# Mixing k and v with tokens on partitions, with crossbar transposes and POOL copies, in a fused attention and feed-forward kernel

## The chip, the cores and the metric

The kernel runs on one core of one Trainium2 chip. The metric is device time in microseconds (us): the median of several executions on the chip. A second number, the span, is the time from the first to the last instruction of one profiled execution, some 2 us shorter.

Engines: PE does matmuls (TensorE), PEld loads their weights, ACT is ScalarE, DVE is VectorE, POOL is GpSimd, SP is the queue that issues most transfers here. Each works off a queue of its own. In this kernel the order on PE, POOL and SP is fixed by hand, and the traces below show POOL and SP keeping to it: a kT copy starts only behind a gate and its loads (at 125.49 us), a transpose of v only behind one of q (at 77.47 us).

## The reference, cut to what matters

```python
B, H, S, D = 4, 8, 768, 64;  n_blocks = 8;  block = 96
P = sort_net                                   # [B, H, 8, 8], five normalising rounds (cut)
k_sorted = einsum('bhij,bhjcd->bhicd', P, k_b) # every block becomes a mix of the 8 blocks
v_sorted = einsum('bhij,bhjcd->bhicd', P, v_b)
scores = scale * q_b @ k_sb.T;  attn = softmax(scores) @ v_sb     # per block of 96 tokens
x = attn as [3072, 512];  out = ((x @ w_a) * (x @ w_b)) @ w_out   # d_ff = 1536
```

## The kernel before

Heads are worked on in pairs: batch `b` has pairs `g = 4b .. 4b+3`. Batch 0 has a path of its own. While PE does the feed-forward of batch `b`, small units of the attention of batch `b+1` are put between its steps. A unit is `c_` (mix k and v), `s_` (scores and exponentials) or `o_` (output). A gate is a POOL copy of one element: POOL waits for its source, and so the loads that follow it in program order are held back. In the views `pf` and `po` are the matmuls of the first and second half of the feed-forward, `mix`, `sc` and `o_ps` those of the three units; `hT` holds what lies between the two halves.

```python
def stage_mix(g, what, engines):               # 12 matmuls, 128 columns each, for k or for v
    mix = psA.tile([P, 2, 512], FP32, tag="A", name="mix")
    for c in range(NCH):                       # NCH = 6
        for e in range(2):                     # the two heads: lower and upper half of the array
            nc.tensor.matmul(mix[e * D:(e + 1) * D, c // 3, c % 3 * P:(c % 3 + 1) * P],
                             lhsT=src2[:, e, c * D:(c + 1) * D], rhs=s_all[:, 2 * g + e], ...)
    ...                                        # copied to kT or vT: d on partitions, tokens along
    if what == "v" and g > HP:                 # HP = 4
        nc.sync.dma_start_transpose(out=vss[g % NBUF][:, :, V0:V0 + P], in_=...)

def c_(g):
    ...
    stage_mix(g, "k", ("act",))
    stage_mix(g, "v", ("dve", "act"))
    if 2 * HP - 2 <= g < B * HP - 2:           # pace the loads of the pair after next
        nc.gpsimd.tensor_copy(out=gate, in_=kTs[g % NBUF][0:1, 0:1])
        load_pair((g + 2) // HP, (g + 2) % HP) # k, v, q: three loads issued by POOL

def s_(g):
    stage_scores(g)
    ...
    pair_q(g + 1)                              # POOL copy of q (qc)
    stage_q(g + 1)                             # crossbar transpose of it (qTf), on SP

for u, n in ((c_, 0), (s_, 0), (c_, 1), (s_, 1), (c_, 2), (o_, 0), (s_, 2), (c_, 3),
             (o_, 1), (s_, 3), (o_, 2), (o_, 3)): ...
```

The softmax here doesn't subtract the row's maximum and nothing guards it: scores larger than these inputs give would overflow.

## Time and profile before

| | before |
|---|---|
| time, median of 3 first runs | 245.47 us (245.16 to 245.64) |
| span of the profiled run | 243.3 us |
| PE busy | 237.4 us, 98% |
| mean granted TensorE clock | 1.0 |
| PE waits in the steady part | 0.2 us |

The page of the kernel before, its busy times (us, share of the span, instructions) and the chain of work that ended last, by engine and by line:

```profile
PE 237.4 (98%) x2309; PEld 141.6 (58%) x2309; DVE 109.1 (45%) x258; ACT 104.4 (43%) x204; POOL 61.4 (25%) x88
...
PE 93%; DVE 4%; ACT 1%; DMA 1%; issue 0%
PE pf L332 52%; PE po L377 24%; PE mix L281 4%; PE o_ps L231 3%; PE sc L302 2%; PE mixh L180 2%; PE po L362 1%; PE vs_ps L208 1%; PE xt_ps L222 1%; PE sc L195 1%; DMA p_nat<-in_sort_net_dram 1%; PE heat L168 1%; PE two L332 1%; PE q_ps L260 1%; DVE xp L237 1%
```

PE is the bound: its instructions fill 93% of the chain. The mixes are 4% of it. Everything else hides behind PE, as long as PE never waits.

The same chain in order of time (start, length, what), at the start of batch 2's attention:

```profile
84.17 1.30 PE pf L332 x8
85.47 0.79 PE mix L281 x24
86.26 2.71 PE pf L332 x16
88.97 0.45 PE sc L302 x16
```

A mix of one pair takes 0.79 us, and the 16 matmuls behind it 2.71 us where 16 undisturbed ones take 2 x 1.30. So a mix costs 0.90 us in all. The scores stand one short stretch of feed-forward behind.

The timeline of POOL of the kernel before, for one mixing unit (start, length, what, and in brackets its idle time before with the releaser):

```profile
102.53 0.18 POOL L542 COPY gate<-kT 1x1 bf16<-1x1 bf16 x1 [4.45 <-ACT kT L162]
103.04 0.72 POOL L95 DMA_DIRECT2D k<-in_k_dram  x1 [0.34 <-PE pf L332]
103.75 0.72 POOL L95 DMA_DIRECT2D v<-in_v_dram  x1
104.46 0.73 POOL L95 DMA_DIRECT2D q<-in_q_dram  x1
105.18 0.85 POOL L246 COPY qc<-q 128x768 bf16<-128x768 bf16 x1
```

From the gate to the end of the third load issue POOL is held for 2.65 us. Before the change no score waits for POOL: kT is written by ACT, and the POOL copies of q come early enough.

### The profile page before, as it was taken

Reading aid. Unit: us, or ns where it says so; the run is one execution under the profiler, and the core shown is the slowest. Engines: PE = TensorE matmul, PEld = TensorE weight load, DVE = VectorE, ACT = ScalarE, POOL = GpSimd, SP = SyncE. Lnnn points to the kernel's source line nnn. Section 1 sums busy time; section 2 is a strip of 40 time slices with the busy share of each in tenths; the row PEclk is TensorE's granted clock in tenths of the full one; section 3 lists DMA queues with packets and bytes.
Section 4 is the critical chain, followed back from the end, with each engine's and each line's share of the span. In section 5 each row is a group of like instructions: output and inputs, shape, how many; then the busy total and the mean of one; then the engine's idle time right before and its main releaser. Section 6 shows DMA issues by size and latency. Waiting matters only on the chain.

```text
span 243.3 us, 5625 instructions
## 1 busy us (share of the span) xinstructions
PE 237.4 (98%) x2309; PEld 141.6 (58%) x2309; DVE 109.1 (45%) x258; ACT 104.4 (43%) x204; POOL 61.4 (25%) x88
## 2 busy tenths in 40 slices
PE   7999999999999999999999999999999999999994
PEld 7776666666554466666654466666654466665442
DVE  6774557555435234464534144363625144344110
ACT  3675853565630175736330165737330133333001
POOL 8766569623220053240400054200000000000000
PEclk9999999999999999999999999999999999999999
DMA  5999999985999589993964369923524310000132
GB/s 78 202 198 196 196 201 201 203 138 83 158 204 153 130 70 155 171 138 70 136 115 122 115 120 114 159 51 58 47 75 131 109 43 0 3 0 1 46 129 86
DMA packets 53930, 28.04 MB, mean 115 GB/s; under 512 B 30736, under 2 KB 50960, under 8 KB 53904
## 3 DMA queue, kind: packets, MB, share of 16 engines
q0 software_dynamic: 20944, 14.16, 41.6%
q1 hardware_dynamic: 32816, 13.45, 28.0%
q8 instruction: 18, 0.29, 0.5%
q14 instruction: 8, 0.07, 0.1%
q10 hardware_dynamic: 144, 0.07, 0.1%
HBM read 28.32 MB, written 6.29 MB: 142 GB/s over the span
## 4 chain that ended last, share of the span: by engine, by line
PE 93%; DVE 4%; ACT 1%; DMA 1%; issue 0%
PE pf L332 52%; PE po L377 24%; PE mix L281 4%; PE o_ps L231 3%; PE sc L302 2%; PE mixh L180 2%; PE po L362 1%; PE vs_ps L208 1%; PE xt_ps L222 1%; PE sc L195 1%; DMA p_nat<-in_sort_net_dram 1%; PE heat L168 1%; PE two L332 1%; PE q_ps L260 1%; DVE xp L237 1%
## 5 line engine op out<-in xcount | busy, mean ns | idle before, releaser
L353 DVE TENSOR_TENSOR hT<-a_sb,pf 128x384 bf16<-128x384 bf16 x95 | 52.6, 553 | 73.8 <-PE pf L332 46.4
L332 PE MATMUL pf<-xT,w_a_sb 128*128 128x384 bf16 x380 | 78.0, 326 | 0.2 <-ACT xT L162 0.2
L332 PE MATMUL pf<-xT,w_b_sb 128*128 128x384 bf16 x380 | 77.5, 326 | 0.0
L352 ACT CAST a_sb<-pf 128x384 bf16<-128x384 f32 x95 | 45.5, 479 | 60.9 <-PE pf L332 41.3
L377 PE MATMUL po<-w_out_sb,hT 128*128 128x512 bf16 x276 | 61.9, 379 | 0.0
L332 PEld LDWEIGHTS <-w_b_sb 128*128 128x128 bf16 x384 | 37.5, 98 | 24.8 <-issue 0.3
L332 PEld LDWEIGHTS <-w_a_sb 128*128 128x128 bf16 x384 | 34.9, 98 | 22.2
L377 PEld LDWEIGHTS <-hT 128*128 128x128 bf16 x276 | 26.3, 98 | 30.0
L162 ACT COPY o_sb<-po 128x512 f32<-128x512 f32 (+1 forms) x13 | 7.5, 577 | 46.8 <-PE po L377 45.2
L164 DVE COPY o_sb<-po 128x512 f32<-128x512 f32 (+1 forms) x12 | 7.9, 656 | 35.2 <-PE po L377 26.3
L307 ACT ACTIVATE eT<-sc 96x768 bf16<-96x768 f32 x24 | 18.0, 802 | 6.9 <-PE sc L302 6.9
L542 POOL COPY gate<-kT 1x1 bf16<-1x1 bf16 x8 | 1.4, 179 | 74.7 <-ACT kT L162 74.7
L237 DVE TENSOR_TENSOR xp<-o_ps,rec 96x512 bf16<-96x512 f32 x24 | 15.9, 684 | 0.6 <-DVE rec L235 0.2
L162 ACT CAST kT<-mix 128x384 bf16<-128x384 f32 x24 | 10.3, 482 | 8.0 <-PE mix L281 8.0
L95 POOL DMA_DIRECT2D k<-in_k_dram x16 | 11.6, 724 | 4.5 <-PE pf L332 2.3
L95 POOL DMA_DIRECT2D v<-in_v_dram x16 | 11.5, 721 | 3.1 <-DMA w_b_sb<-in_moe_w_b_dram 1.2
L231 PEld LDWEIGHTS <-eT 96*128 96x128 bf16 x256 | 10.4, 97 | 3.2 <-DVE xp L237 0.6
L235 DVE RECIPROCAL rec<-o_ps 96x8 f32<-96x8 f32 x32 | 5.6, 189 | 13.8 <-PE o_ps L231 13.8
L231 PE MATMUL o_ps<-vs,eT 96*128 96x65 bf16 x256 | 11.3, 193 | 0.2 <-DVE xp L237 0.2
L246 POOL COPY qc<-q 128x768 bf16<-128x768 bf16 x10 | 8.4, 842 | 7.2 <-DMA q<-in_q_dram 7.2
L95 POOL DMA_DIRECT2D q<-in_q_dram x12 | 8.7, 721 | 1.7 <-DMA w_a_sb<-in_moe_w_a_dram 0.7
L168 PE MATMUL heat<-warm 128*128 128x128 bf16 x84 | 7.6, 264 | 1.3 <-DVE warm L77 1.3
(80 smaller groups left out, 158.3 us busy)
## 6 DMA issues: line engine op xcount, KB each, us to landing
out_dram<-o_sb SPq DMA_DIRECT2D x17, 256.0 KB, 2.0
k<-in_k_dram POOLq DMA_DIRECT2D x16, 192.0 KB, 6.0
v<-in_v_dram POOLq DMA_DIRECT2D x16, 192.0 KB, 6.4
q<-in_q_dram POOLq DMA_DIRECT2D x12, 192.0 KB, 6.7
w_a_sb<-in_moe_w_a_dram POOLq DMA_DIRECT2D x6, 256.0 KB, 9.8
w_b_sb<-in_moe_w_b_dram POOLq DMA_DIRECT2D x6, 256.0 KB, 10.0
w_out_sb<-in_moe_w_out_dram POOLq DMA_DIRECT2D x3, 512.0 KB, 10.8
out_dram<-o_sb SPq DMA_DIRECT2D x12, 128.0 KB, 2.4
```

What stands on the lines that cost most here:

```text
L95: nc.gpsimd.dma_start(out=to, in_=_ap(t, base, [[W, P], [S * D, 2], [1, W]]))
L162: nc.scalar.copy(out=out, in_=in_)
L168: nc.tensor.matmul(ps[:, 0:cols], lhsT=warm[:, 0:P], rhs=warm[:, 0:cols], start=True, stop=True)
L231: nc.tensor.matmul(o_ps[:, e, i * (D + 1):(i + 1) * (D + 1)], lhsT=eT[:, hf, e, i * BLK:i * BLK + P], rhs=vs[0:BLK, i0 + i, V0 - 1 + e * ( ...
L237: nc.vector.tensor_tensor(out=_ap(xp, i0 * 2 * D, [[nxp * 2 * D, BLK], [D, 2], [2 * D, NBH], [1, D]]), in0=_ap(o_ps, 1, [[1024, BLK], [511 ...
L246: nc.gpsimd.tensor_copy(out=qc.rearrange("p c e d -> p e c d"), in_=loaded[g][2].rearrange("p e (c d) -> p e c d", c=NCH))
L281: nc.tensor.matmul(mix[e * D:(e + 1) * D, c // 3, c % 3 * P:(c % 3 + 1) * P], lhsT=src2[:, e, c * D:(c + 1) * D], rhs=s_all[:, 2 * g + e], ...
L307: nc.scalar.activation(out=eT[:, hf, :, 0:HB], in_=sc[0:BLK, :, 0:HB], func=AF.Exp, scale=float(scale))
L332: nc.tensor.matmul(pf[:, 0:HW], lhsT=w_sb[:, kc, m * P:(m + 1) * P], rhs=x_cols(b, kc, t), start=(kc == 0), stop=(kc == KA - 1))
L352: nc.scalar.copy(out=a_sb, in_=pf[:, 0:HW])
L353: nc.vector.tensor_mul(out=hT[:, m, t * HW:(t + 1) * HW], in0=a_sb, in1=ab[1][:, 0:HW])
L377: nc.tensor.matmul(held["po"], lhsT=hTs[b][:, m, c * P:(c + 1) * P], rhs=w_out_sb[:, m, :], start=(m == 0), stop=(m == KO - 1))
```

## The change: intent and diff

The intent is to take PE work away. With tokens on partitions one mix is 2 matmuls of 384 columns with the mixing matrix as weights, in place of 12 of 128 columns. The result then has to be turned: k by one crossbar transpose, v by two, and POOL copies put the blocks in order. The mix of the next pair moves ahead of the scores, to give this longer path time. One buffer of hT goes, for space. Core of the diff:

```diff
+    def stage_kv(g):
+        for n, (what, engines) in enumerate((("k", ("act",)), ("v", ("dve", "act")))):
+            ...
+            for e in range(2):
+                nc.tensor.matmul(mix[:, e, 0:W], lhsT=s_all[:, 2 * g + e], rhs=src2[:, e], ...)
+            nat = att.tile([P, NCH, 2, D], BF16, tag="nat", name="nat")
+            ...                                   # copies mix -> nat on ACT, or DVE and ACT
+            nc.sync.dma_start_transpose(out=turned, in_=nat.rearrange("p c e d -> p (c e d)"))
+    def order_kv(g):                              # two POOL copies: turned -> kT, turned -> vT
+        for what, to in (("k", kTs[...]...), ("v", vTs[...]...)):
+            nc.gpsimd.tensor_copy(out=to, in_=st[g, what].rearrange("p c (i t) -> p c i t", i=NB))
+    def return_v(g):                              # the transpose of v that was there before
-            hTs[b] = ffp.tile([P, KO, S], BF16, tag="hT", name="hT")
+            hTs[b] = ffp.tile([P, KO, S], BF16, tag="hT", name="hT", bufs=1)
 def c_(g):
-                stage_mix(g, "k", ("act",))
-                stage_mix(g, "v", ("dve", "act"))
+                if g > HP:
+                    stage_kv(g)
+                else: ...                         # as before
                 if 2 * HP - 2 <= g < B * HP - 2:
-                    nc.gpsimd.tensor_copy(out=gate, in_=kTs[g % NBUF][0:1, 0:1])
+                    nc.gpsimd.tensor_copy(out=gate, in_=st[g, "v", "nat"][0:1, 0, 0, 0:1])
                     load_pair((g + 2) // HP, (g + 2) % HP)
-            for u, n in ((c_, 0), (s_, 0), (c_, 1), (s_, 1), (c_, 2), (o_, 0), (s_, 2), (c_, 3),
-                         (o_, 1), (s_, 3), (o_, 2), (o_, 3)):
+            # (unit, pair, what follows it, for which pair)
+            for u, n, then, m in ((c_, 0, None, 0), (c_, 1, order_kv, 0), (s_, 0, return_v, 0),
+                                  (c_, 2, order_kv, 1), (s_, 1, return_v, 1), (o_, 0, None, 0),
+                                  (c_, 3, order_kv, 2), (s_, 2, return_v, 2), (o_, 1, order_kv, 3),
+                                  (s_, 3, return_v, 3), (o_, 2, None, 0), (o_, 3, None, 0)):
```

It touches 11 pairs: 5 to 15.

More of the change, by code (lines that the diff above doesn't have):

```diff
@@ L290, in stage_mix @@
                 copy(eng, d1, s1)
-        if what == "v" and g > HP:
-            nc.sync.dma_start_transpose(out=vss[g % NBUF][:, :, V0:V0 + P],
-                                        in_=to.rearrange("p i t -> p (i t)"))
+    def stage_kv(g):
+        for n, (what, engines) in enumerate((("k", ("act",)), ("v", ("dve", "act")))):
+            src2 = loaded[g][n]
+            mix = psA.tile([P, 2, 512], FP32, tag="A", name="mix")
+            for e in range(2):
+                nc.tensor.matmul(mix[:, e, 0:W], lhsT=s_all[:, 2 * g + e], rhs=src2[:, e],
+                                 start=True, stop=True)
+            nat = att.tile([P, NCH, 2, D], BF16, tag="nat", name="nat")
+            step = 2 // len(engines)
+            for u, eng in enumerate(engines):
+                copy(eng, nat[:, :, u * step:(u + 1) * step].rearrange("p c e d -> p e c d"),
+                     mix[:, u * step:(u + 1) * step, 0:W].rearrange("p e (c d) -> p e c d", c=NCH))
+            turned = att.tile([P, NCH, P], BF16, tag="turned", name="turned")
+            nc.sync.dma_start_transpose(out=turned, in_=nat.rearrange("p c e d -> p (c e d)"))
+            st[g, what, "nat"], st[g, what] = nat, turned
+    def order_kv(g):
+        for what, to in (("k", kTs[g % NBUF][:, 0:S].rearrange("p (i c t) -> p c i t", i=NB, c=NCH)),
+                         ("v", vTs[g % NBUF][:, :, 0:BLK].rearrange("p i (c t) -> p c i t", c=NCH))):
+            nc.gpsimd.tensor_copy(out=to, in_=st[g, what].rearrange("p c (i t) -> p c i t", i=NB))
+    def return_v(g):
+        nc.sync.dma_start_transpose(out=vss[g % NBUF][:, :, V0:V0 + P],
+                                    in_=vTs[g % NBUF].rearrange("p i t -> p (i t)"))
     def stage_scores(g):
@@ L538, in c_ @@
                     turn_q(g)
-                stage_mix(g, "k", ("act",))
-                stage_mix(g, "v", ("dve", "act"))
+                if g > HP:
+                    stage_kv(g)
+                else:
+                    stage_mix(g, "k", ("act",))
+                    stage_mix(g, "v", ("dve", "act"))
                 if 2 * HP - 2 <= g < B * HP - 2:
-                    nc.gpsimd.tensor_copy(out=gate, in_=kTs[g % NBUF][0:1, 0:1])
+                    nc.gpsimd.tensor_copy(out=gate, in_=st[g, "v", "nat"][0:1, 0, 0, 0:1])
                     load_pair((g + 2) // HP, (g + 2) % HP)
@@ L557, in o_, with run @@
                 to_xT(g)
-            for u, n in ((c_, 0), (s_, 0), (c_, 1), (s_, 1), (c_, 2), (o_, 0), (s_, 2), (c_, 3),
-                         (o_, 1), (s_, 3), (o_, 2), (o_, 3)):
-                us.append(lambda u=u, g=g0 + n: u(g))
+            def run(u, g, then, n):
+                u(g)
+                if then is not None and g0 + n > HP:
+                    then(g0 + n)
+            for u, n, then, m in ((c_, 0, None, 0), (c_, 1, order_kv, 0), (s_, 0, return_v, 0),
+                                  (c_, 2, order_kv, 1), (s_, 1, return_v, 1), (o_, 0, None, 0),
+                                  (c_, 3, order_kv, 2), (s_, 2, return_v, 2), (o_, 1, order_kv, 3),
+                                  (s_, 3, return_v, 3), (o_, 2, None, 0), (o_, 3, None, 0)):
+                us.append(lambda u=u, g=g0 + n, then=then, m=m: run(u, g, then, m))
             return us
```

## The prediction

> **What bounds the kernel now.** TensorE. The page of busy times gives PE 237.4 us of 243.3 (98%); the chain that ended last lies on PE for 93% of the span, and the granted clock is 1.0. The feed-forward matmuls are 76% of that chain (52% pf, 24% po); the k and v mix is 4%. Almost no PE wait is left in it. DVE (45%), ACT (43%) and POOL (25%) have room. So two things count: PE time removed, and new waits of PE.
>
> **What it removes.** For 11 of 12 later pairs, 24 mix matmuls of 128 columns become 4 of 384. Columns streamed hardly change: the old ones run two side by side in column halves. The chain shows 0.79 us for an old pair of mixes, and the 8 pf matmuls behind them take 1.41 us where undisturbed ones take 1.30: 0.90 in all. Eight 384-column matmuls take 1.30, so four should take 0.65. Saving about 0.25 us x 11 = 2.7 us. Evacuations keep their sizes (ACT 0.48, DVE 0.56 us).
>
> **What it adds.** Per pair two crossbar transposes on SP (1.23 us issue; existing ones land in 2.8 us when the DMA is quiet, 5.8 median, up to 7.6 with loads running) and two POOL copies of 128x768 (the like-sized qc copy takes 0.84 us). Single-buffered hT should cost nothing.
>
> **What lies on the critical path.** Not the mean load but the order on POOL. order_kv of pair n-1 is queued behind the next pair's gate and its three load issues. The timeline shows 2.65 us from gate start to the end of the third issue. The gate now waits for DVE's v evacuation, about 1.45 us after the mix starts. So kT is ready about 1.45 + 2.65 + 0.85 = 5.0 us after the next pair's mix starts. The scores that need it are planned only 1, 2 or 3 steps of 1.3 us behind that mix, at 1.95, 3.25 or 4.55 us. Waits: 3.05, 1.75, 0.45 us. Six gated cases: batch 1, 1.75 + 3.05; batch 2, 0.45 + 1.75 + 1.75; batch 3, 0.45. Sum 9.2 us. The DMA is already 90% busy in much of 40 to 110 us; two more transposes a pair make landings later, so the first scores of batch 2 and the last return of v in batch 1 may wait another 1 to 3 us. I take 11 to 12 us of new PE waits.
>
> The Trainium skill (DMA: Bandwidth & Descriptors, "Issuing engine by pattern") lets transposes run only from hardware queues; the trace agrees, all 33 are on SP. So one that waits for POOL holds back those queued behind it.
>
> **Predicted time.** 245.5 - 2.7 + 11.7 = 254.5 us, range 247.5 to 264. Faster by over 2%: 0.02; within 2%: 0.2; slower: 0.78.
>
> **What would show each step.** PE mix per changed pair near 0.65 us, with 1.30 behind it. New idle time of PE or its weight load before the scores, released by POOL's kT copy, 5 to 12 us in about six pieces, in batch 2 at its first three score stages, in batch 3 almost none after the first. POOL busy up about 19 us. Share of the hardware queue up from 28% to about 40%; median landing of transposes above 5 us.
>
> **What would make it wrong.** POOL copies with 16-element runs slower than 0.84 us (each 0.4 us more adds about 2.5 us). Landings so late that DMA holds the scores (worse). The other way: a gate released earlier than I think, or waits that absorb each other, leaves only the PE saving and the time within 2%.

## The result, and the profile after

| | before | after |
|---|---|---|
| time, median | 245.54 us (4 runs) | 259.37 us (257.8 to 262.81, 4 runs, one of them slow) |
| ratio of the fast runs, 95% interval | | 1.0545 (1.0459 to 1.0631) |
| span of the profiled run | 243.3 us | 256.2 us |
| mean granted clock | 1.0 | 0.993 |

All ratios here are taken from fast runs alone, so not quite the ratio of the quoted medians. The mean of the three fast runs is 258.84 us. An execution counts as slow when it is more than 1.5% above the fastest one of its kernel.

The same parts of the page, of the changed kernel:

```profile
PE 235.9 (92%) x2078; PEld 139.2 (54%) x2089; DVE 109.3 (43%) x258; ACT 104.0 (41%) x193; POOL 78.8 (31%) x110
...
PE 73%; DMA 11%; POOL 6%; DVE 4%; issue 2%; ACT 2%; SPq 1%; POOLq 0%; DVEq 0%
```

PE is busy 1.5 us less, yet the span grew by 12.9 us. The chain now runs through DMA and POOL for 17%. So PE waits. Its largest waits in the changed kernel (who waited for whom: us in total, times, longest):

```profile
PE sc L324 <- POOL kT L311: 7.0, 5, 2.9
PE sc L324 <- DMA qTf<-qc: 4.7, 2, 3.4
PE o_ps L231 <- DMA vs<-vT: 2.4, 1, 2.4
```

That is 14.1 us in eight pieces. The timeline of PE of the changed kernel shows where each stands (only the lines with a wait in brackets):

```profile
58.34 0.51 PE L324 MATMUL sc<-qT,kT 64*128 64x96 bf16 x16 [1.66 <-POOL kT L311]
...
68.22 0.51 PE L324 MATMUL sc<-qTf,kT 64*128 64x96 bf16 x16 [2.93 <-POOL kT L311]
...
80.74 0.65 PE L231 MATMUL o_ps<-vs,eT 96*128 96x65 bf16 x16 [2.37 <-DMA vs<-vT]
...
99.92 0.51 PE L324 MATMUL sc<-qTf,kT 64*128 64x96 bf16 x16 [0.36 <-POOL kT L311]
...
111.13 0.82 PE L324 MATMUL sc<-qTf,kT 64*128 64x96 bf16 x16 [3.44 <-DMA qTf<-qc]
...
126.41 0.51 PE L324 MATMUL sc<-qTf,kT 64*128 64x96 bf16 x16 [1.69 <-POOL kT L311]
...
160.58 0.51 PE L324 MATMUL sc<-qTf,kT 64*128 64x96 bf16 x16 [0.38 <-POOL kT L311]
...
169.62 0.52 PE L324 MATMUL sc<-qTf,kT 64*128 64x96 bf16 x16 [1.26 <-DMA qTf<-qc]
```

The first three are in batch 1, the next three in batch 2, the last two in batch 3. The timeline of POOL of the changed kernel, just ahead of the wait at 126.41:

```profile
122.90 0.18 POOL L567 COPY gate<-nat 1x1 bf16<-1x1 bf16 x1 [10.91 <-DVE nat L164]
123.35 0.72 POOL L95 DMA_DIRECT2D k<-in_k_dram  x1 [0.28 <-issue]
124.07 0.72 POOL L95 DMA_DIRECT2D v<-in_v_dram  x1
124.78 0.73 POOL L95 DMA_DIRECT2D q<-in_q_dram  x1
125.49 0.86 POOL L311 COPY kT<-turned 128x768 bf16<-128x768 bf16 x1
```

POOL was idle for 10.91 us before the gate. The kT copy stood in line behind a gate that waits for the mix of the next pair, and behind three load issues.

The chain in order of time of the changed kernel, around the longest wait:

```profile
101.42 9.58 DMA qTf<-qc
...
111.13 0.82 PE sc L324 x16
111.96 5.11 PE pf L354 x24
```

Here a transpose of q took 9.58 us from its issue to its landing. And the 24 matmuls behind the wait took 5.11 us in place of 4.0, the 16 of the scores 0.82 in place of 0.51. The table by stretches explains that (from:to, length, busy time and count of PE, PEld, DVE, ACT and POOL, then the granted clock, the DMA share, which counts packet times and can pass 1, and GB/s):

```profile
111.90:117.00 5.10, 5.10 (x29) 2.83 (x28) 1.11 (x2) 2.71 (x5) 0.09 (x1) 0.78 1.60 160
```

The granted clock was 0.78 there; in 100 to 107 us, up to just before the wait, it was 1.00. The Trainium skill (TensorE: Matmul & The Clock Gate, "What's actually happening") says that an idle window of about 3.4 us takes PE to half clock. This wait of 3.44 us agrees (the clock was 0.50 from 111.13 to 113.0 us); a run below does not.

The mix itself, in the chain of the changed kernel:

```profile
53.43 0.65 PE mix L297 x4
54.08 2.61 PE pf L354 x16
```

0.65 us in place of 0.79, and no 0.11 us lost behind it. The Trainium skill (TensorEngine Tiling (Array Packing), "Key Properties") states that a change of tiling mode drains TensorE. The 0.11 us agrees: it stands behind the mixes that split the array in column halves, and not behind the new ones. The scores, which use half of the rows, are followed by it too: 24 matmuls take 4.01 us behind them, 3.90 behind a new mix (e2). That the drain is its cause is not shown; no run isolates it.

The sum: waits of 14.1 us, less about 2.5 us of mix (measured below), plus 1.4 us at the lower clock (1.1 in the 24 matmuls, 0.3 in the scores before them), make 13.0 us; the span grew by 12.9.

The wait for v has a path of its own. The chain of the changed kernel ahead of it:

```profile
75.43 0.58 SPq L412
...
76.10 1.28 SPq L252
...
77.47 3.13 DMA vs<-vT
```

The POOL copy of this v had ended by 72.94 us. Its transpose was issued at 77.47, behind an output store (L412) and the next q transpose (L252) on SP's queue, and then landed in 3.1 us, as fast as any of v. Issued at once it would have landed at about 76.1 (an estimate from these numbers), and PE asked for it at 78.37. So I read this wait of 2.4 us as one of place on SP's queue, not of a late landing; no run moves that transpose alone.

### The profile page after: what moved, and what is told of

Its sections match the earlier page's. It is cut to its first block, busy times and chain, and to the rows that moved or that the text cites. A ratio compares the mean times of both kernels' runs of the same rounds, so it can differ in the third digit from the quotient of the medians.

```text
span 256.2 us, 5237 instructions
## 1 busy us (share of the span) xinstructions
PE 235.9 (92%) x2078; PEld 139.2 (54%) x2089; DVE 109.3 (43%) x258; ACT 104.0 (41%) x193; POOL 78.8 (31%) x110
## 3 DMA queue, kind: packets, MB, share of 16 engines
q1 hardware_dynamic: 50416, 17.78, 38.7%
## 4 chain that ended last, share of the span: by engine, by line
PE 73%; DMA 11%; POOL 6%; DVE 4%; issue 2%; ACT 2%; SPq 1%; POOLq 0%; DVEq 0%
PE pf L354 38%; PE po L399 22%; DMA qTf<-qc 6%; PE o_ps L231 3%; DMA turned<-nat 2%; PE mix L297 2%; PE sc L324 2%; PE mixh L180 2%; POOL q L95 1%; POOL kT L311 1%; DMA vs<-vT 1%; POOL k L95 1%; PE po L384 1%; PE vs_ps L208 1%; PE xt_ps L222 1%
## 5 line engine op out<-in xcount | busy, mean ns | idle before, releaser
L354 PEld LDWEIGHTS <-w_a_sb 128*128 128x128 bf16 x384 | 36.0, 98 | 23.0 <-issue 0.5
L567 POOL COPY gate<-nat 1x1 bf16<-1x1 bf16 x8 | 1.4, 179 | 69.0 <-DVE nat L164 69.0
L162 ACT CAST nat<-mix 128x768 bf16<-128x768 f32 (+1 forms) x22 | 14.1, 639 | 7.3 <-PE mix L297 5.0
L324 PE MATMUL sc<-qTf,kT 64*128 64x96 bf16 x160 | 5.6, 211 | 10.1 <-POOL kT L311 5.4
L324 PEld LDWEIGHTS <-kT 64*128 64x128 bf16 x192 | 4.8, 97 | 16.4 <-POOL kT L311 8.9
L311 POOL COPY kT<-turned 128x768 bf16<-128x768 bf16 x11 | 9.3, 842 | 11.4 <-PE pf L354 10.1
```

The costliest lines, as they stand in the source:

```text
L162: nc.scalar.copy(out=out, in_=in_)
L311: nc.gpsimd.tensor_copy(out=to, in_=st[g, what].rearrange("p c (i t) -> p c i t", i=NB))
L324: nc.tensor.matmul(sc[:, e, i * BLK:(i + 1) * BLK], lhsT=kT[e * D:(e + 1) * D, blk * BLK:blk * BLK + P], rhs=qT[e * D:(e + 1) * D, :, blk ...
L354: nc.tensor.matmul(pf[:, 0:HW], lhsT=w_sb[:, kc, m * P:(m + 1) * P], rhs=x_cols(b, kc, t), start=(kc == 0), stop=(kc == KA - 1))
```

## The experiments

Two theories stood against each other for the waits. A: the place on POOL's queue; the kT copy stands behind the next pair's gate and loads. B: the crowded DMA; transposes land late beside the loads, whatever the order. C, a relative of A, says the q transposes are late because of where their copy stands on POOL. Eleven kernels ran. e1, e4, e5 and e6 ran on one chip, with 245.07 us before (7 runs).

### e1: the block-order copies ahead of gate and loads

```diff
 def c_(g):
     ...                                # stage_kv
+    if g > HP + 1 and g % HP > 0:
+        order_kv(g - 1)
     if 2 * HP - 2 <= g < B * HP - 2:   # gate, load_pair
-(c_, 1, order_kv, 0) (c_, 2, order_kv, 1) (c_, 3, order_kv, 2)
+(c_, 1, None, 0)     (c_, 2, None, 1)     (c_, 3, None, 2)
```

> The changed kernel with one move: on POOL the two block-order copies of the pair before go ahead of the gate and the three load issues, not behind them. Theory A (order on the POOL queue: 2.65 us of gate and load issues stand between the gate and the kT copy): the five waits of the scores for POOL's kT copy, 7.0 us in the profile of after, go nearly all; the waits for the q transposes (4.7 us) and for v (2.4 us) stay; about 251 us (249 to 253.5). Rival B (the DMA is crowded, transposes land late whatever the order on POOL): the waits come back with the landing of the transposes as the releaser, and the time stays at 256 or above.

Measured: 252.19 us (251.45 to 252.78, 4 fast runs), ratio 1.0287 (1.0263 to 1.0311). The waits of PE:

```profile
PE o_ps L231 <- DMA vs<-vT: 3.5, 1, 3.5
PE sc L324 <- POOL kT L311: 2.3, 1, 2.3
PE sc L324 <- DMA qTf<-qc: 1.8, 1, 1.8
PE sc L324 <- POOL qc L246: 1.7, 1, 1.7
```

The time is A's. The excess over before fell from 5.45% to 2.87%. Four of the five waits for kT are gone; the one left is in batch 1, where the copy itself had waited 3.98 us for the transpose to land. So A holds for these waits. About 9 us of waits remain, all behind transposes from SP's queue. The profile puts one of them, 1.7 us, down to the q copy, but that copy is for the pair after; the q transpose which those scores need landed 6.0 us after its issue, at 108.9 us, just ahead of them (109.09). So it is a q wait too.

### e4: e1 without the later loads (wrong result)

```diff
-                    load_pair((g + 2) // HP, (g + 2) % HP)
+                    loaded[g + 2] = loaded[(g + 2) % HP + HP]
```

> Wrong result on purpose: e1 with the eight later loads of k, v and q left out (pairs 8 to 15 use the data of pairs 4 to 7), so that neither their issues nor their DMA traffic is there; all transposes stay. Theory A: the loads' harm was their place on the POOL queue, which e1 has already mended, so this is within 1.5 us of e1. Rival B: with the loads' traffic gone the transposes land in about 3 us instead of 5 to 12, all waits for q and v go too, and the time falls to 243 to 245, 6 us or more below e1.

Measured: 245.54 us (245.0 to 246.12), ratio 1.001 (0.9984 to 1.0035), so 6.7 us under e1. One wait of the steady part is left, 2.4 us for v. The issues of the profile (what, queue, count, median us to landing):

```profile
turned<-nat SPq DMA_TRANSPOSE x22, 2.8
...
vs<-vT SPq DMA_TRANSPOSE x11, 3.1
qTf<-qc SPq DMA_TRANSPOSE x10, 2.8
```

Without the loads the new transposes land in 2.8 us; in the changed kernel their median was 5.3 and the longest 12.8. So B holds for most of what e1 left: this is the half that A does not explain. e4 takes the load issues from POOL's queue as well as the traffic; e7 parts the two. B had the wait for v go too, and that failed: it is as long as in the changed kernel, with the transposes of v landing in 3.1 us. Even so the kernel only draws level with before: the v wait of batch 1 and moments at a lower clock (0.992 in the profile) eat the saving.

### e7: the changed kernel, POOL copies in place of the loads (wrong result)

```diff
                     nc.gpsimd.tensor_copy(out=gate, in_=st[g, "v", "nat"][0:1, 0, 0, 0:1])
-                    load_pair((g + 2) // HP, (g + 2) % HP)
+                    for _ in range(3):
+                        nc.gpsimd.tensor_copy(out=pad, in_=q_first[:, 0:2, 0:320])
+                    loaded[g + 2] = loaded[(g + 2) % HP + HP]
```

> Wrong result on purpose: the changed kernel in its own order, its later loads replaced by three POOL copies of 128x640 (about 0.73 us each by the 0.84 us of a 128x768 one), so POOL is held as long at the same place but the loads' traffic is gone. The counterpart of e4 (no loads, order mended: 245.5). Theory A, that the place on POOL costs by itself: the waits for POOL's kT copy return in full, 1.7, 2.9, 0.4, 1.7, 1.7 and 0.4 us, about 8 us in sum, and with the v wait that e4 kept the time is 251 to 255. Rival B, that only the loads' traffic hurts: within 1.5 us of e4, 244 to 247.

Measured, where before was 245.05 us (11 runs): 253.01 us (251.19 to 254.75), ratio 1.0318 (1.0276 to 1.0359). It was run at another time. A stand-in copy took 0.716 us, a load issue 0.72. The waits of PE:

```profile
PE sc L325 <- POOL kT L312: 6.5, 4, 2.6
PE o_ps L232 <- DMA vs<-vT: 2.3, 1, 2.3
```

A's waits are back, 6.5 us of them (1.28, 2.58, 1.33 and 1.33; about 8 expected, and the two of 0.4 did not come), with no later load traffic at all. The last but one is the wait that the q transpose hid in the changed kernel. Theory B, that only the traffic hurts, falls. But there is no wait for q any more, although the copy of q for the second scores of batch 2 starts as late (5.4 us after the mix of its own pair starts, 5.7 in the changed kernel): the q transposes land in 2.7 to 2.9 us. So the q waits come from the traffic, not from the place of the copy. C falls in that form, B holds for q.

One line goes against the page quoted above. After a wait of 2.58 us (before 67.82) the clock was low:

```profile
67.80:72.00 4.20, 4.07 (x27) 2.09 (x29) 0.56 (x1) 1.98 (x3) 3.10 (x4) 0.59 0.42 77
```

After the 2.35 us for v it was 0.50 from 81.9 to 85 us. In the changed kernel waits of 2.93 and 2.37 us left the clock at 1.00. So a wait shorter than 3.4 us may or may not cost clock. The runs do not show what decides it.

### e5: q earlier on top of e1

```diff
+                if 2 * HP <= g and g + 1 < B * HP:
+                    pair_q(g + 1); stage_q(g + 1)    # behind order_kv, ahead of gate and loads
```

(and taken out of `s_`).

> e1 with the q copy and the q transpose of the next pair moved up as well: ahead of the gate and loads, one mixing stage earlier than before. Theory C (the q transposes come late because their copy waits on POOL's queue behind block-order copies that wait for landings, and behind load issues): the two q waits of 4.7 us go, 3 to 5 us less than e1, about 247. Rival B (landings limited by the DMA): the q transposes are issued earlier but land as late, time as e1 within 1.5 us.

Measured: 249.14 and 252.51 us in fast runs, two slow ones at 252.9 and 253.0; ratio 1.0233 (1.0151 to 1.0314), called unclear. It doesn't settle C.

### e10: q earlier alone, in the changed kernel

The same move without e1, so q goes ahead of gate, loads and the block-order copies.

> The changed kernel with the q copy and q transpose of the next pair moved ahead of the gate and loads, one mixing stage earlier; the block-order copies stay behind the loads. Theory C (the two q waits, 4.7 us, come from where the q copy stands on POOL, behind loads and block-order copies): the waits for q transposes go, the hidden wait for the kT copy in the second scores of batch 2 comes out at about 1.7 us, the other kT waits stay at 1.7, 2.9, 0.4, 1.7 and 0.4; about 3 us less than the change, 256 (254.5 to 258). Rival B (transposes land late wherever they are issued): q waits of 3 us or more stay, time 257.5 to 261 as the change itself.

Measured: 274.15 us (4 runs, one of them slow), ratio 1.1166 (1.1126 to 1.1207), far outside both expectations. The timeline of POOL:

```profile
97.21 0.72 POOL L95 DMA_DIRECT2D q<-in_q_dram  x1
105.28 0.82 POOL L246 COPY qc<-q 128x768 bf16<-128x768 bf16 x1 [7.35 <-DMA q<-in_q_dram]
...
108.31 0.84 POOL L311 COPY kT<-turned 128x768 bf16<-128x768 bf16 x1
```

I had moved the q copy so early that it waits for a load issued just ahead of it. POOL stood still for 7.35 us with the kT copy in line behind, and PE waited 8.21 us for it (22.0 us for kT copies in all). No wait for q is left, so one half of C's expectation came true, but the edit changed more than the thing it was to test. As a test of C it is void; as a measurement of what a blocked head of a queue costs it is clear.

### e6: the loads moved to the end of each batch

e5, with the four pairs of the next batch loaded in the last four units (`o_1, s_3, o_2, o_3`) of the batch before.

> e5 with the later loads taken out of the mixing stages: the four pairs of the next batch are loaded during the last four units of the batch before, when fewer transposes run. Same number of instructions and bytes as the change. If queue order and the overlap of loads with transposes together are the whole loss, PE waits of stages are under 1.5 us in sum and the time is that of before less the saving of the mix, 242.5 to 245. If rival B holds in the sense that five transposes a pair are too many for the DMA at any time, waits of 3 us or more remain and it is over 248.

Measured: 261.34 us (4 runs, one of them slow), ratio 1.0635 (1.0576 to 1.0694): worse than the change, and neither theory's figure. In the profile all waits of scores are gone, as A and B both ask. Two new ones took their place; the chain in order of time shows the first:

```profile
71.44 10.44 DMA vs<-vT
...
82.01 1.04 PE o_ps L231 x16
83.05 11.49 PE po L399 x42
```

Three loads of 192 KB were issued in the 2.3 us ahead of this transpose of v, and six more while it ran; it landed after 10.44 us, and PE waited 8.3 us. Then 42 matmuls took 11.49 us, where the same 42 take 9.07 in the kernel before: from 82 to 95 us the granted clock was 0.78. The second wait, 4.7 us, is for an xT transpose among the loads for the batch after that (11.33 us). The Trainium skill (DMA: Bandwidth & Descriptors, "Issuing engines are not separate DMA queues") says that transfers of all queues run on the same 16 DMA engines and interleave. This trace agrees: a transpose from SP's queue took 10.44 us among loads from POOL's, 3.1 in e4 without. I read from it that what counts for a transpose is how much load is in flight around it. No run changes the burst alone; e8 below, which spreads the same bytes, changes other things too.

### e2 and e3: the saving, and the rest of the change, by themselves

e2 is the kernel before with the new matmul shape for pairs 5 to 15 and nothing else (wrong result):

```diff
+        if g > HP:
+            for e in range(2):
+                nc.tensor.matmul(mix[:, e, 0:W], lhsT=s_all[:, 2 * g + e], rhs=src2[:, e], ...)
+        else: ...                       # the 12 matmuls as before
```

> Wrong result on purpose: the kernel before with one edit, the mixes of pairs 5 to 15 done as 4 matmuls of 384 columns; copies, transposes, order of units and hT buffers as before. It measures the saving by itself. My sum: 0.90 - 0.65 = 0.25 us a pair, 11 pairs, 2.7 us less: 242.4 (241.9 to 243.0). Rival: PE streams the same columns, so no saving beyond 0.5 us: 244.5 or more.

Measured: 242.65 us (242.43 to 243.16), ratio 0.9899 (0.9882 to 0.9916). The span fell from 243.3 to 240.8. So the saving is real, 2.4 to 2.5 us, some 0.22 us a pair. With no wait added, it is also the most that this change could have given: 1%.

e3 is the kernel before with the new order of units and one hT buffer.

> The kernel before with the change's order of units (the mix of the next pair ahead of the scores) and the single hT buffer, and nothing else. I expect no cost: 245.1 plus or minus 0.7. If the order of units or the hT buffer were a cause of the loss, it is 247 or more.

Measured: 245.74 us in the median of 8 runs, ratio 1.0019 (1.0001 to 1.0036). Six runs lie at 245.26 to 246.25; of the other two 247.78 counts as fast and 250.04 as slow. Mostly as expected: not a cause of 5%. Its profile is of the slow run, so it explains no time. But it shows that a q transpose can be late without the new transposes: the one for the second scores of batch 2 took 10.46 us, and PE waited 2.54 us. The new order of units puts the loads of two pairs, six, ahead of that transpose, where the kernel before has three (5.8 us to landing there). How much of the q waits of the changed kernel is due to that is untested.

### e8, e9, e11: a version that beats both

If A and B are both right, the new mix pays where its long path has time, its copies stand first on POOL, and loads come in small doses. e8 takes the new path for batches 2 and 3 only (8 pairs), and loads one tensor a unit:

```diff
 def c_(g):
+    if g >= 2 * HP:
+        stage_kv(g)
+        if g % HP > 0: order_kv(g - 1)           # first on POOL
+        pair_q(g); stage_q(g)
+    else: ...                                    # as before the change, old order of units
+todo = {2: [[(10, 0), (10, 1)], [(10, 2)], [(11, 0)], ...], 3: [[(14, 1)], [(14, 2)], ...]}
+# after unit j: a gate on that unit's own result, then load_one(pair, k or v or q) for todo[j]
```

> A try at a version that beats both: the new path for batches 2 and 3 only (8 pairs, so batch 1 with its short stages is as before), block-order copies ahead of everything else on POOL, q copy and transpose in the pair's own mixing stage, and the later loads issued one tensor a unit, not three or more at once. If both causes (place on POOL, bursts of loads ahead of transposes) are right, waits of PE at scores and outputs sum to under 1 us and the time is that of before less 8 x 0.25 us: 243.2 (242.5 to 245). If the DMA as such is too full for five transposes a pair beside loads, waits for q, k or v landings of 3 us or more stay and it is over 246.

Measured: 245.81 us, ratio 1.0036 (1.0009 to 1.0063). Only 2.0 us of waits were left, both for the q transpose of a batch's first pair. e9 moves those to the end of the batch before:

```diff
 def o_(g):
+    if g % HP == HP - 1 and g + 1 < B * HP:
+        pair_q(g + 1); stage_q(g + 1)
-todo = {2: [[(10, 0), (10, 1)], [(10, 2)], ...
+todo = {2: [[(10, 0)], [(10, 1), (10, 2)], ...
```

> The spread version again, with the q copy and q transpose of each batch's first pair moved to the end of the batch before (the only PE waits that were left in its profile were 1.81 and 0.20 us, both for the q transpose of a batch's first pair), and one load tensor moved one unit later. If that was all, no PE wait before scores over 0.3 us is left and the time is that of before less 8 x 0.22 us: 243.3 (242.8 to 244.2). If the next transposes in the queue merely take over the wait, 245 or more.

Measured: 244.18 us, ratio 0.9961 (0.9947 to 0.9974). One wait was left, 0.77 us for v of pair 10, the load I had put later. e11 puts that load back:

```diff
-todo = {2: [[(10, 0)], [(10, 1), (10, 2)], ...
+todo = {2: [[(10, 0), (10, 1)], [(10, 2)], ...
```

> The best version so far (244.2) with one load, v of pair 10, issued one unit earlier again, because its profile shows one PE wait of 0.77 us for that load. If the rest stays as it is: 243.4 (243.0 to 244.0), 0.6 to 0.7% under the kernel before. If the two loads side by side push a transpose back into PE's way: 244.2 or more.

Measured: 243.14 us (243.04 to 243.24, 6 fast runs), correct, ratio 0.9912 (0.9897 to 0.9927). The largest waits of PE in its profile:

```profile
PE heat L174 <- DVE warm L77: 1.3, 1, 1.3
PE heat L453 <- DVE rsum L451: 0.4, 2, 0.2
```

The waits that are left lie in the opening, as in the kernel before. It is 2.05 us faster than before (245.19 in those rounds). Eight pairs at the 0.22 us that e2 measured make 1.8; the rest is not explained, and since e11 changes several things at once it does not say what each is worth. The interval lies clear of 1.

## Why the prediction was right or wrong

The time was right in direction and within the range (254.5 us, 247.5 to 264; measured 259.4, or 258.8 as the mean of the fast runs). The range was wide, and its parts were not equally good.

- **The saving.** Predicted 2.7 us, from 0.90 less 0.65 us a pair. e2 measured 2.4 to 2.5. Right.
- **The place on POOL.** Predicted waits of 1.75 and 3.05 in batch 1, 0.45, 1.75 and 1.75 in batch 2, 0.45 in batch 3. The profile has 1.66, 2.93, 0.36, then a q wait of 3.44 that hides one, 1.69 and 0.38: 7.0 us in place of 9.2, the rest hidden. Right, and shown twice: e1 takes most of them away by order alone, e7 brings them back without traffic.
- **The crowded DMA.** Predicted 1 to 3 us, at the first scores of batch 2 and the last return of v in batch 1. The waits for transfers were 7.1 us: 4.7 for q and 2.4 for v. This is the term that was mis-sized. The first scores of batch 2 waited for no transfer. I had not counted the q transposes: they were there before and had just enough time, so I saw them only as a rival. Batch 3, for which I predicted almost no wait after the first scores, waited 1.26 us for q. Without the later loads the q waits go, in e4 and in e7. The wait for v came where I had named it (2.37 us), but not for my reason: it stays without the loads, 2.4 us in e4 and 2.3 in e7, and the chain puts it down to the place on SP's queue. That part was luck.
- **The clock.** Not predicted. A wait of 3.44 us was followed by a stretch at 0.78; with the scores ahead of it that cost another 1.4 us. In all the waits were 14.1 us in place of 11.7, the clock cost 1.4 and the saving was about 0.2 less: 4 us, of the 4.3 by which the fast runs lie above 254.5.
- **Side marks.** POOL busy rose by 17.4 us (19 predicted). The hardware queue's share rose from 28.0% to 38.7% (40 predicted). The new transposes landed in 5.3 us in the median (above 5 predicted), but those of q and v in 4.3 and 3.8, no later than before (4.6 and 5.8): single ones came late. The copies with 16-element runs took 0.84 us, the same as the q copy. The order of units and the single hT buffer cost nearly nothing by themselves in six of the eight runs of e3 (at most 1.2 us above the median before); what they do beside the new transposes is untested.

## What to carry to other kernels

When work moves off the engine that bounds the kernel, follow the new path through every queue it joins, in program order, and ask what stands in front of it there and what that is waiting for. A new copy at the end of a busy engine's queue can cost more than the work that it saves, even where that engine is idle for most of the time. Transfers on which a matmul waits should meet few bytes in flight: spread bulk loads thinly, and look first at old transfers that had just enough time.

## What the Trainium skill lacked or had wrong

- DMA: Bandwidth & Descriptors ("DMA Transpose (X-bar)" and "Latency and other measured facts") gives a bandwidth but no latency for a crossbar transpose. Here a 128x768 one landed in 2.8 us with little else in flight, 5.3 us in the median beside loads, 12.8 at most. It held SP's queue for 1.2 us in the shortest case; the longest on that queue was one of v, 4.7 us.
- The same page ("Issuing engines are not separate DMA queues") says that queues interleave, but not how long a transfer behind a burst takes: 10.4 and 11.3 us amid bursts of loads of 192 KB (e6), against 2.8 to 3.1 without loads (e4).
- TensorE: Matmul & The Clock Gate puts the fall of the clock at an idle window of about 3.4 us. In e7 the granted clock fell to 0.59 (mean of 4.2 us) after a wait of 2.58 us, and to 0.50 (for 3.1 us) after one of 2.35; in the changed kernel it stayed at 1.00 after one of 2.93.
- DMA: Bandwidth & Descriptors ("Anatomy of one DMA — SWDGE (gpsimd) path") puts the dispatch of a load issued by POOL at about 50 ns and calls descriptor generation small and variable. Here each issue of a 192 KB load held POOL's queue for 0.72 us, as long as a 128x640 copy (0.716 us), and three in a row were 2.2 of the 2.65 us that the kT copy stood behind.
